# RWKV-6 recurrence and hard-swish MLP in one kernel: chunks of two batches in turn, first diagonal sums on TensorE, first w loaded by itself, part of the first block's down projection by block products

## The chip, the cores and the metric

The kernel runs on one core of a Trainium2 chip. The metric is the device time of one execution in microseconds, given as the median of several runs. A core has five engines that run side by side, each through its own queue in order: TensorE (PE in the profile; PEld is its loading of stationary operands), VectorE (DVE), ScalarE (ACT), GpSimd (POOL) and SyncE (SP), which here issues nearly all transfers. Products land in PSUM, from where DVE and ACT take them to SBUF.

## The reference

```python
batch, n_heads, seq, head_dim = (4, 8, 768, 48)
for t in range(S):
    kt, vt, rt, wt = (k[:, :, t], v[:, :, t], r[:, :, t], w[:, :, t])
    cur = np.einsum('bhd,bhe->bhde', u[None] * kt, vt)
    y[:, :, t] = np.einsum('bhd,bhde->bhe', rt, state + cur)
    state = wt[:, :, :, None] * state + np.einsum('bhd,bhe->bhde', kt, vt)
...
x = attn_out.transpose(0, 2, 1, 3).reshape(B * S, H * D)   # 3072 x 384
h = x @ w_in                                                # 384 x 2048
relu6 = np.clip(h + 3.0, 0.0, 6.0)
g = h * relu6 / 6.0
return (g @ w_out).astype(np.float32)                       # 2048 x 384
```

All of r, k, v, w, u are float32; the two weight matrices come as float64.

## The kernel before

**Chunks and blocks.** The 768 steps of a batch are cut into 6 chunks of 128 (L), which makes 24 chunks, numbered in the order of the batches: chunks 0 to 5 are batch 0. A chunk is a row tile of 128 tokens of the MLP as well, and four chunks (BC) make a block of 512 tokens; there are six blocks.

**A chunk of the recurrence.** Its steps in the planner's list (lines 769 to 832), with the chunk's number behind the name:

- `feat` loads r, k and w with the head's dimension on partitions (674 KB; for chunk 0 in two parts, w on SP's queue and r and k on ACT's, with u's broadcast behind them, L257 to L259), `tok` loads r, k and v with time on partitions (576 KB, L267).
- `back` (DVE, a scan of w from the end, L333, and a reciprocal, L337), `fore` (DVE, a scan from the start, L342), `K` and `R` (products of k and r with the two scans, L353 and L357; on DVE for the first three chunks, on GpSimd then).
- `own` makes r*k*u for the diagonal (two multiplications, L366 and L367, on DVE for chunk 0 and on GpSimd for the others), `sum` reduces it over the head's dimension (DVE, L372), `diag0` and `diag1` lay the result on the diagonals of A (ACT, L380, eight instructions).
- `score` (PE, L388) makes the products of K and R, `above` (DVE, L395, two instructions) puts the part above the diagonal into A.
- `turn` and `turned` transpose K (PE L404, ACT L409), `read` multiplies the state (L440) and the values (L457) into y_ps and makes the chunk's own contribution to the state (L450), `state` (DVE, L414 or L416) adds it, and `decay` (L421) multiplies the state before by the chunk's decay. A batch's first chunk has no state to read, its last none to write. Chunk i's decay needs the state of chunk i-1.
- `leave` copies y_ps into xT, the operand of the MLP. In block 0 a chunk is read in two steps: `first` and `third` take the last pair of heads out (L480), `read` adds it back by a selection product (L487), and `leave` is one copy (L496). In later blocks three small transfers per half (`move`, L517) place the last pair.

**Weights.** Sixteen pairs of weight tiles are fetched as 64-bit words (`fetch`, L292, 768 KB each, three buffers `bits`) and turned into float32: `low` and `whole` on ACT (L301, L305), `shift`, `join` and `full` on DVE (L310, L315, L320).

**Block 0** uses the weights as they arrive. `up` (PE, L536) makes one column tile f of 128 of the hidden layer for one half p of the block (two chunks), 16 x 2 times; `ramp` (ACT, L526) and `gate` (DVE, L544) make the activation into g0 or g1, one tile for each half of the block. `down` (PE, L552) multiplies g of one chunk with w_out, 16 column tiles of 128 in eight steps of two, `drain` (ACT, L559) scales the result and `store` writes it. Blocks 1 to 5 use products of 2 x 2 blocks with seven instead of eight products (`up_product` L634, `down_product` L681), which need sums of blocks of the weights (`sin` L594, `sout` L606), of x (`tx`, L616) and of g (`sum`, L666), and add the products up when they are read out of PSUM (L643, L645, L694, L696).

**The order of the work** is written out by the program before it is built: each step has an engine, a length, the steps it waits for, a key, buffers that it holds (`ring`), and for a load its size. A planner (class Plan) runs through modelled time and takes, of the steps that can start first on an engine, the one with the lowest key. START, CONV, UP, SUMS and LAG give the keys of the first chunks, the conversions, block 0's up steps, the weight sums, and how long before a block its last chunk is read; BEHIND says which weight fetch a chunk's loads come after. Until the first `up` PE runs filler products (`spin`, L980) where the planner sees it without work. Every engine then runs its list in order, whatever the real times are.

Of the kernel before, what the change touches and what calls it, by code (L numbers as in the profile page):

```python
# [18 lines left out]
L = 128  # L19
GP = 64  # L20
LEVELS = 7
BC = 4
# [3 lines left out]
LAG = 19.1  # L26
BEHIND = (-1, -1, 0, 3, 5, 8)
EARLY = 3
START = (-104.5, -104.0, -78.0, -38.2, 22.0, 30.0)
CONV = (-90.0, 6.6)  # L30
UP = (-83.9, 3.6, -69.0, 4.3)
SUMS = (36.2, 2.0)
# [148 lines left out]
def fast_path(tc, feat, tok, wflat, ub, moe_w_in, moe_w_out, out, flag, n_chunks):  # L181
# [20 lines left out]
    with ExitStack() as ctx:  # L202
# [5 lines left out]

        plan = Plan()
# [10 lines left out]
        states = [const.tile([PR, P, D], F32, name=f"state_{i}") for i in range(2)]  # L220
        u_bc = const.tile([128, HD], F32, name="u_bc")
# [32 lines left out]
        def load_feat(i):  # L254
            a = io.tile([PR, nf], F32, name="feat_in")
            if i == 0:
                nc.sync.dma_start(out=a[:, 2 * n:], in_=feat[i, :, 2 * n:])  # L257
                nc.scalar.dma_start(out=a[:, :2 * n], in_=feat[i, :, :2 * n])
                nc.scalar.dma_start(out=u_bc, in_=ub.to_broadcast([128, HD]))  # L259
            else:  # L260
                nc.sync.dma_start(out=a, in_=feat[i])
            st[i].update(r=a[:, :n].rearrange("q (p t) -> q p t", p=P),
                         k=a[:, n:2 * n].rearrange("q (p t) -> q p t", p=P), w=a[:, 2 * n:])

        def load_tok(i):
            b = io.tile([L, 3, HD], F32, name="tok_in", bufs=3)
            nc.sync.dma_start(out=b.rearrange("s c e -> s (c e)"), in_=tok[i].rearrange("s c e -> s (c e)"))  # L267
            st[i].update(rt=b[:, 0], kt=b[:, 1], v=b[:, 2].rearrange("s (h d) -> s h d", d=D))
# [93 lines left out]
        def own(i):  # L362
            d = st[i]
            d["rk"] = wk.tile([L, HD], F32, name="rk", bufs=1)
            eng = nc.vector if i == 0 else nc.gpsimd
            eng.tensor_mul(d["rk"], d["rt"], d["kt"])  # L366
            eng.tensor_mul(d["rk"], d["rk"], u_bc)  # L367

        def own_sum(i):
            d = st[i]  # L370
            d["dg"] = wk.tile([L, H, 1], F32, name="dg")
            nc.vector.tensor_reduce(out=d["dg"].rearrange("s h o -> s (h o)"),  # L372
# [38 lines left out]
        def new_state(i):  # L411
            d = st[i]
            if i % n_chunks == 0:
# [4 lines left out]
        def decay(i):  # L418
            d = st[i]
            d["S"] = wk.tile([PR, P, D], F32, name="S")  # L420
            early(i).tensor_mul(d["S"], states[(i - 1) % 2], d["E"][:, :, 0:1].to_broadcast([PR, P, D]))  # L421
# [12 lines left out]
        def read_state(i, pairs):  # L434
            d = st[i]
            if i % n_chunks:
# [5 lines left out]
        def write(i):  # L442
            d = st[i]
            if i % n_chunks != n_chunks - 1:
# [75 lines left out]
        def new_g(bk, p):  # L520
            blocks[bk]["g", p] = wk.tile([128, NFC, HB], F32, name=f"g{p}", bufs=1)
# [10 lines left out]
        def up(f, p):  # L532
            b = blocks[0]
            h_ps = b["h", f, p] = bank("bankA" if f % 2 else "bankC")
            for j in range(NCC):
                nc.tensor.matmul(h_ps[:, :HB], lhsT=w_in[:, f // 2, j, f % 2, :], rhs=b["xT"][:, j, p * HB:(p + 1) * HB],  # L536
                                 start=(j == 0), stop=(j == NCC - 1))

        def ramp(f, p):
            clip(0, p, blocks[0]["h", f, p][:, :HB], ("r", f, p))  # L540

        def gate(f, p):
            b = blocks[0]
            nc.vector.scalar_tensor_tensor(out=b["g", p][:, f, :], in0=b["r", f, p][:, :HB], scalar=6.0,  # L544
                                           in1=b["h", f, p][:, :HB], op0=ALU.min, op1=ALU.mult)

        def down(c, f0, f1):
# [3 lines left out]
            for f in range(f0, f1):  # L551
                nc.tensor.matmul(b["o", c][:, :DM], lhsT=b["g", c // 2][:, f, c % 2 * L:(c % 2 + 1) * L], rhs=w_out[:, f, :],  # L552
# [8 lines left out]
        def store(bk, c):  # L561
            t0 = bk * MB + c * L
# [92 lines left out]
        def sum_g(bk, p, k, x):  # L655
# [6 lines left out]
            G = b["g", p].rearrange("q f (c t) -> q f c t", c=2)  # L662
# [656 lines left out]
```

## Time and profile before

| | us |
|---|---|
| median of 6 runs | 584.48 (583.68 to 585.09) |
| the profiled execution | 585.28 |
| its span, first to last instruction | 583.6 |
| PE busy | 568.0 (97%) |
| DVE busy | 401.5 (69%) |
| ACT busy | 265.4 (45%) |
| GpSimd busy | 129.0 (22%) |
| mean granted TensorE clock | 0.993 |

The costliest groups of PE are the block products (L634 and L681), then block 0's down projection (L552, 128 passes, 44.4 us of busy time). A float32 product is two passes in the trace, so a product counts as two instructions. Shares of busy time are averages over stages that differ: the first 73 us of the span hold the loads, the conversion of the weights and the first chunks, and the rest is one stream of products. In the views below, a row of stages gives start and end, length, and the busy time of PE, PEld, DVE, ACT and POOL with the number of instructions, and then the granted clock, the busy share of the 16 DMA engines and GB/s. A row of waits reads: the engine and line that waited, who released it, the microseconds in total, how many times, and the longest. A row of a timeline has start, length, engine, line, operation, tiles and, in brackets, the idle time before it and what ended it.

### The profile page before, as it was taken

To read this page: it belongs to the slowest core of one execution; us is meant where nothing else is said; L and a number is where in the kernel's file an instruction comes from. 1 tells how busy PE (TensorE), PEld (TensorE's weight loads), DVE (VectorE), ACT (ScalarE), POOL (GpSimd) and SP (SyncE) were. 2 spreads that over 40 slices of the span, in tenths; PEclk is the share of its full clock that TensorE was granted. 3 is DMA by queue.
4 is the path that set the end of the run, shared out by engine and by line. 5 is a ranking of instruction groups with operands and counts; after the bars stand their busy time and mean duration, and the time that the engine had idled before them with its cause. 6 is when DMAs were issued, how large, how long until landed. Compare 5 with 4: busy or idle time off the path is not lost.

```text
span 583.6 us, 10098 instructions
## 1 busy us (share of the span) xinstructions
PE 568.0 (97%) x3940; PEld 497.1 (85%) x3940; DVE 401.5 (69%) x666; ACT 265.4 (45%) x677; POOL 129.0 (22%) x119
## 2 busy tenths in 40 slices
PE   8997899999999999999999999999999999999995
PEld 8776687666888999988899988899988899988995
DVE  7998798896787996587788477878365634155350
ACT  3677683434656512457630457530456510265100
POOL 3212215435504213304231503142211000000000
PEclk9998999999999999999999999999999999999999
DMA  8969651534324544534437333542100000100001
GB/s 273 334 194 303 195 197 48 172 129 140 125 60 145 198 120 152 181 102 123 164 113 233 122 103 102 152 145 78 64 6 8 2 8 15 43 1 0 1 15 46
DMA packets 20777, 67.26 MB, mean 115 GB/s; under 512 B 2752, under 2 KB 6912, under 8 KB 20720
## 3 DMA queue, kind: packets, MB, share of 16 engines
q1 hardware_dynamic: 20448, 65.86, 34.8%
q8 instruction: 33, 0.54, 0.4%
q10 hardware_dynamic: 272, 0.66, 0.4%
q14 instruction: 24, 0.20, 0.1%
HBM read 60.81 MB, written 4.72 MB: 112 GB/s over the span
## 4 chain that ended last, share of the span: by engine, by line
PE 92%; DVE 4%; DMA 1%; ACT 1%; issue 0%; SPq 0%; DVEq 0%
PE bankA L634 18%; PE bankA L681 17%; PE bankC L634 9%; PE bankC L681 9%; PE bankA L552 7%; PE bankB L634 6%; PE bankB L681 4%; PE y_ps L457 4%; PE bankC L536 4%; PE bankB L388 4%; PE bankA L536 4%; PE y_ps L440 2%; PE ps L450 2%; PE ps L404 1%; DMA tok_in<-in_tok_dram 1%; PE bankA L980 1%
## 5 line engine op out<-in xcount | busy, mean ns | idle before, releaser
L643 ACT COPY g<-bankA 128x256 f32<-128x256 f32 x120 | 44.5, 371 | 51.7 <-PE bankA L634 49.3
L653 DVE SCALAR_TENSOR_TENSOR g<-clip,g 128x512 f32<-128x512 f32 x80 | 58.1, 729 | 9.8 <-ACT clip L526 9.8
L380 ACT ACTIVATE A<-ident,dg 128x128 f32<-128x128 f32 x192 | 59.8, 391 | 10.4 <-DVE dg L372 8.8
L526 ACT ACTIVATE clip<-g,three 128x512 f32<-128x512 f32 x80 | 57.9, 723 | 11.3 <-DVE g L645 10.6
L634 PE MATMUL bankA<-xT,w_in 128*128 128x256 f32 x240 | 60.9, 381 | 0.0
L421 POOL TENSOR_TENSOR S<-state,E 112x192 f32<-112x192 f32 x18 | 19.0, 1058 | 178.3 <-DVE state L416 115.0
L681 PE MATMUL bankA<-w_out,g 128*128 128x192 f32 x320 | 56.8, 328 | 0.0
L681 PEld LDWEIGHTS bankA<-w_out,g 128*128 128x128 f32 x320 | 52.5, 190 | 1.0 <-issue 0.4
L634 PEld LDWEIGHTS bankA<-xT,w_in 128*128 128x128 f32 x240 | 45.0, 190 | 6.0 <-issue 0.4
L552 PE MATMUL bankA<-w_out,g 128*128 128x384 f32 x128 | 44.4, 494 | 1.4 <-DVE w_out L320 1.4
L634 PE MATMUL bankB<-xT,w_in 128*128 128x256 f32 x160 | 41.3, 381 | 0.0
L357 POOL TENSOR_TENSOR W<-feat_in,W 112x512 f32<-112x512 f32 x21 | 27.4, 1303 | 57.2 <-DVE W L342 24.7
L510 ACT COPY xT<-y_ps 48x384 f32<-48x384 f32 x40 | 18.9, 472 | 45.7 <-PE y_ps L457 45.3
L366 POOL TENSOR_TENSOR rk<-tok_in 128x384 f32<-128x384 f32 x23 | 27.0, 1172 | 52.6 <-DMA tok_in<-in_tok_dram 33.6
L694 ACT ACTIVATE o<-bankA 128x192 f32<-128x192 f32 x30 | 9.9, 330 | 62.6 <-PE bankA L681 62.6
L353 POOL TENSOR_TENSOR E<-feat_in,E 112x512 f32<-112x512 f32 x21 | 27.5, 1311 | 45.2 <-issue 34.8
L552 PEld LDWEIGHTS bankA<-w_out,g 128*128 128x128 f32 x128 | 23.5, 190 | 16.4 <-DVE w_out L320 1.6
L645 DVE TENSOR_TENSOR g<-bankC,g 128x256 f32<-128x256 f32 x40 | 16.9, 421 | 26.7 <-PE bankC L634 24.6
L645 DVE TENSOR_TENSOR g<-bankB,g 128x256 f32<-128x256 f32 x40 | 16.9, 421 | 25.0 <-PE bankB L634 22.4
L634 PEld LDWEIGHTS bankB<-xT,w_in 128*128 128x128 f32 x160 | 30.3, 190 | 4.3 <-issue 0.2
L342 DVE TENSOR_TENSOR_SCAN W<-feat_in,start 112x516 f32<-112x516 f32 x24 | 33.2, 1383 | 0.1
L333 DVE TENSOR_TENSOR_SCAN E<-feat_in,back 112x516 f32<-112x516 f32 x24 | 29.4, 1224 | 2.6 <-DMA feat_in<-in_feat_dram 2.6
(260 smaller groups left out, 1248.8 us busy)
## 6 DMA issues: line engine op xcount, KB each, us to landing
feat_in<-in_feat_dram SPq DMA_DIRECT2D x23, 674.2 KB, 4.7
tok_in<-in_tok_dram SPq DMA_DIRECT2D x24, 576.0 KB, 4.3
bits<-in_moe_w_in_dram SPq DMA_DIRECT2D x8, 768.0 KB, 8.5
bits<-in_moe_w_out_dram SPq DMA_DIRECT2D x8, 768.0 KB, 4.5
feat_in<-in_moe_w_in_dram SPq DMA_DIRECT2D x8, 768.0 KB, 4.2
feat_in<-in_moe_w_out_dram SPq DMA_DIRECT2D x8, 768.0 KB, 4.4
out_dram<-o SPq DMA_DIRECT2D x24, 192.0 KB, 1.9
feat_in<-in_wflat_dram SPq DMA_DIRECT2D x6, 768.0 KB, 4.4
```

The costliest lines, as they stand in the source:

```text
L333: nc.vector.tensor_tensor_scan(out=E_[:, ::-1], data0=d["w"][:, :0:-1], data1=back.rearrange("q p t -> q (p t)")[:, ::-1], initial=0.0, op ...
L342: nc.vector.tensor_tensor_scan(out=W_, data0=d["w"][:, :-1], data1=starts[i % 2].rearrange("q p t -> q (p t)"), initial=0.0, op0=ALU.mult, ...
L353: early(i).tensor_mul(d["K"], d["k"], d["K"])
L380: nc.scalar.activation(out=d["A"][:, h, :], in_=ident, func=ACT.Copy, scale=d["dg"][:, h])
L526: nc.scalar.activation(out=c[:, :m], in_=src, func=ACT.Relu, bias=three, scale=1.0)
L536: nc.tensor.matmul(h_ps[:, :HB], lhsT=w_in[:, f // 2, j, f % 2, :], rhs=b["xT"][:, j, p * HB:(p + 1) * HB], start=(j == 0), stop=(j == NCC ...
L552: nc.tensor.matmul(b["o", c][:, :DM], lhsT=b["g", c // 2][:, f, c % 2 * L:(c % 2 + 1) * L], rhs=w_out[:, f, :], start=(f == 0), stop=(f == ...
L634: nc.tensor.matmul(b["p", q, to][:, :HB], lhsT=w, rhs=rhs, start=(n == 0 and k in (1, 2, 5)), stop=(n == len(terms) - 1 and k in (2, 3, 4) ...
L643: nc.scalar.copy(out=to, in_=src)
L645: nc.vector.tensor_add(to, src, to)
L653: nc.vector.scalar_tensor_tensor(out=g, in0=b["r", q, p], scalar=6.0, in1=g, op0=ALU.min, op1=ALU.mult)
L681: nc.tensor.matmul(b["d", p, to][:, :h], lhsT=a, rhs=w(), start=(f == 0 and k in (1, 2, 5)), stop=(f == HF - 1 and k in (2, 3, 4)), skip_g ...
```

## The change

1. **Chunks of two batches in turn.** Chunk i of the program is no longer chunk i of the data: `chunk_of` takes batches 0 and 1 in turn for the first twelve, then 2 and 3. The first two and the last two of each twelve are first and last chunks; `decay` of chunk i needs the state of chunk i-2.
2. **Diagonal sums of chunks 0 to 3 by TensorE.** `own` is one multiplication r*k on DVE in the layout with the head's dimension on partitions, `dot` multiplies it with u on PE (four products of two columns), and `sum` is a copy on ACT. Their `tok` loads v alone (192 KB). u's broadcast is loaded on SP after the fourth weight fetch, for the chunks from 4 on; a small `u_col` is loaded on ACT's queue at the start.
3. **First w alone.** Chunk 0's r and k are loaded on SP after its w, not on ACT's queue beside it.
4. **Down projection of chunks 2 and 3 by block products.** Block 0's second half uses `down_product`, with its sums and reads, in place of 2 x 8 `down` steps. g0 and g1 are laid out by halves of the hidden layer for block 0. A down product waits only for the weight sum that it uses, not for all.
5. **Keys and filler.** LAG, BEHIND, START, CONV, UP and SUMS have other values, the lengths of `up`, `ramp` and `gate` are given by the number of chunks (the same two halves), and ten of the filler products are done as four products of quarters of the array.

```diff
+SPLIT = (2,)
-LAG = 19.1
-BEHIND = (-1, -1, 0, 3, 5, 8)
+LAG = 12.5
+BEHIND = (-1, -1, -1, 0, 6, 7)
+BY_PE = 4
+OWN = 0.5
-START = (-104.5, -104.0, -78.0, -38.2, 22.0, 30.0)
-CONV = (-90.0, 6.6)
-UP = (-83.9, 3.6, -69.0, 4.3)
-SUMS = (36.2, 2.0)
+START = (-119.6, -152.0, -58.6, -43.4, 14.5, 25.8)
+CONV = (-91.7, 6.6)
+UP = (-83.9, 4.3, -71.3, 4.8)
+SUMS = (53.5, 2.3)
...
+        NSEQ = 2 * n_chunks
+        chunk_of = [(i // NSEQ * 2 + i % 2) * n_chunks + i % NSEQ // 2 for i in range(NT)]
+        def is_first(i):
+            return i % NSEQ < 2
+        def is_last(i):
+            return i % NSEQ >= NSEQ - 2
...
             if i == 0:
-                nc.sync.dma_start(out=a[:, 2 * n:], in_=feat[i, :, 2 * n:])
-                nc.scalar.dma_start(out=a[:, :2 * n], in_=feat[i, :, :2 * n])
-                nc.scalar.dma_start(out=u_bc, in_=ub.to_broadcast([128, HD]))
+                nc.sync.dma_start(out=a[:, 2 * n:], in_=feat[chunk_of[i], :, 2 * n:])
+                nc.scalar.dma_start(out=u_col, in_=ug)
...
+        def load_rest():
+            nc.sync.dma_start(out=st[0]["a"][:, :2 * n], in_=feat[chunk_of[0], :, :2 * n])
+        def load_u():
+            nc.sync.dma_start(out=u_bc, in_=ub.to_broadcast([128, HD]))
...
+            if i < BY_PE:
+                nc.sync.dma_start(out=b[:, 2], in_=tok[chunk_of[i], :, 2])
...
         def own(i):
             d = st[i]
+            if i < BY_PE:
+                d["rk"] = wk.tile([PR, P, L], F32, name="rk", bufs=1)
+                nc.vector.tensor_mul(d["rk"], d["r"], d["k"])
+                return
             d["rk"] = wk.tile([L, HD], F32, name="rk", bufs=1)
-            eng = nc.vector if i == 0 else nc.gpsimd
-            eng.tensor_mul(d["rk"], d["rt"], d["kt"])
-            eng.tensor_mul(d["rk"], d["rk"], u_bc)
+            nc.gpsimd.tensor_mul(d["rk"], d["rt"], d["kt"])
+            nc.gpsimd.tensor_mul(d["rk"], d["rk"], u_bc)
+        def own_dot(i):
+            d = st[i]
+            d["dg_ps"] = pp.tile([L, P, 2], F32, name="ps")
+            for p in range(P):
+                nc.tensor.matmul(d["dg_ps"][:, p, :], lhsT=d["rk"][:, p, :], rhs=u_col[:, p, :], start=True, stop=True)
...
+            if i < BY_PE:
+                nc.scalar.copy(out=d["dg"].rearrange("s h o -> s (h o)"), in_=d["dg_ps"].rearrange("s p g -> s (p g)"))
+                return
...
-            early(i).tensor_mul(d["S"], states[(i - 1) % 2], d["E"][:, :, 0:1].to_broadcast([PR, P, D]))
+            early(i).tensor_mul(d["S"], states[i % 2], d["E"][:, :, 0:1].to_broadcast([PR, P, D]))
...
+        def g_of(bk, f, c):
+            if bk == 0:
+                return blocks[0]["g", f // HF][:, f % HF, c * L:(c + 1) * L]
+            return blocks[bk]["g", c // 2][:, f, c % 2 * L:(c % 2 + 1) * L]
...
+            if i < BY_PE:
+                plan.add(f"own{i}", "DVE", 0.66, do(own, i), [f"feat{i}"] + ["later"] * (i == 0) + [f"own{i - 1}"] * (i > 0), k + OWN,
+                         [("rk", [f"dot{i}"])], port=True)
+                plan.add(f"dot{i}", "PE", 0.55, do(own_dot, i), [f"own{i}"], k + OWN, [("ps", [f"sum{i}"])])
+                plan.add(f"sum{i}", "ACT", 0.22, do(own_sum, i), [f"dot{i}"], k + OWN, [("dg", [f"diag1{i}"])])
...
-                         [f"state{i - 1}", f"back{i}"], t - 0.1 if i < len(START) else t - 5, [("S", [f"read{i}"] + [f"state{i}"] * turn)], port=True)
+                         [f"state{i - 2}", f"back{i}"], t - 0.1 if i < len(START) else t - 5, [("S", [f"read{i}"] + [f"state{i}"] * turn)], port=True)
...
-        plan.add("later", "ACT", 0.9, lambda: None, key=-99.0, kb=1, lands=7.2)
+        plan.add("u", "SP", 0.45, load_u, ["fetch3"], -60.0, kb=197)
+        plan.add("later", "SP", 0.45, load_rest, ["feat0"], key=-999.0, kb=459)
...
-        for c in range(BC):
+        for c in classic:
             for q in range(HF):
                 k = D0 + c * D0 / BC + q * 1.29
                 plan.add(f"down0.{c}.{q}", "PE", 1.29, do(down, c, 2 * q, 2 * q + 2),
...
-            for p in range(2):
-                at = K + U_ + D_ * p
+            for p in range(bk == 0, 2):
+                at = K + U_ + D_ * p if bk else D0 * 1.5
...
-                                 before + [d_ + f"{k_}.0"] * x + [d_ + f"{chain}.1"] * bool(chain) + after + sout
-                                 , at + 2.6 * n_ + 1.3 * x + (2.6 if k_ == 4 else 0), hold if x == 0 else ())
+                                 before + [d_ + f"{k_}.0"] * x + [d_ + f"{chain}.1"] * bool(chain) + after + [f"sout{t_}.{x}" for t_ in ({5: 1, 6: 2, 7: 3, 4: 4}.get(k_),) if t_], at + 2.6 * n_ + 1.3 * x + (2.6 if k_ == 4 else 0), hold if x == 0 else ())
...
         def spin():
-            s_ps = bank("bankA")
-            nc.tensor.matmul(s_ps[:, :L], lhsT=ident, rhs=ident, start=True, stop=True)
+            spins.append(len(spins))
+            if 6 <= spins[-1] < 16:
+                two = [bank("bankA") for _ in range(2)]
+                for rows, cols in ((0, 0), (GP, GP), (0, GP), (GP, 0)):
+                    nc.tensor.matmul(two[rows // GP][cols:cols + GP, :GP], lhsT=ident[rows:rows + D, rows:rows + GP],
+                                     rhs=ident[rows:rows + D, rows:rows + GP], start=True, stop=True)
+                return
+            nc.tensor.matmul(bank("bankA")[:, :L], lhsT=ident, rhs=ident, start=True, stop=True)
```

(`classic` is the first two chunks; `all_down` waits for their `down` steps and the seven products of the second half.)

## The prediction

> **What bounds the kernel now.** I read first the 40 slices of the page (each digit is a busy share in tenths):
>
> ```profile
> PE   8997899999999999999999999999999999999995
> ...
> DVE  7998798896787996587788477878365634155350
> ...
> PEclk9998999999999999999999999999999999999999
> DMA  8969651534324544534437333542100000100001
> ```
>
> PE is full from slice 5 on; only the first five slices (73 us) have room, and there DVE and DMA are nearly full too. Next the busy time by stage (length, then PE, PEld, DVE, ACT, POOL, then granted clock, DMA share, GB/s):
>
> ```profile
> 0.00:11.00 11.00, 9.49 (x58) 9.30 (x58) 6.87 (x14) 2.40 (x6) 2.63 (x13) 1.00 0.78 236
> 11.00:28.80 17.80, 16.33 (x184) 13.75 (x182) 16.42 (x23) 12.09 (x31) 5.08 (x4) 1.00 1.03 345
> 28.80:54.00 25.20, 21.25 (x147) 17.18 (x146) 22.33 (x38) 18.67 (x40) 5.94 (x6) 0.99 0.77 248
> 54.00:72.00 18.00, 15.59 (x105) 11.77 (x106) 14.66 (x21) 11.92 (x28) 3.45 (x3) 0.83 0.66 210
> 72.00:101.00 29.00, 29.00 (x136) 23.07 (x135) 26.37 (x44) 17.70 (x36) 10.11 (x7) 1.00 0.38 130
> ```
>
> From 72 us on PE has no gap, so the end moves only by what PE does not do before 72 and by PE work that vanishes. PE's timeline gives the first. The first product of the up projection (L536) starts at 28.75; what PE does before is mostly filler (L980). Adding the start-to-start times of the other rows there (two turns of K 0.4, two scores 1.1, first reads 0.35 and 0.71, selections 0.86 and 0.77, rests 1.25 and 1.82) gives 8.8 us of real work, so 20.0 us are lost. After 28.75 come these waits:
>
> ```profile
> PE bankC L536 <- DVE w_in L320: 3.7, 1, 3.7
> ...
> PE bankA L552 <- DVE w_out L320: 1.4, 1, 1.4
> PE y_ps L487 <- ACT x L480: 1.3, 2, 0.7
> ```
>
> and behind the first of them the clock is at half:
>
> ```profile
> 54.00:58.00 4.00, 3.63 (x9) 2.92 (x10) 3.83 (x6) 2.67 (x8) 0.00 (x0) 0.50 0.87 248
> 58.00:62.00 4.00, 4.00 (x15) 3.35 (x14) 1.25 (x5) 1.55 (x4) 1.81 (x2) 0.71 0.79 281
> ```
>
> Three groups L536 take 6.9 us there (54.37 to 61.26) against 3 x 1.29 = 3.9. So 3.7 + 3.0 + 1.4 + 1.3 = 9.4 us are lost in the middle, 29.4 in all. Why PE waited at 50.7 is seen on DVE:
>
> ```profile
> 51.25 0.42 DVE L544 SCALAR_TENSOR_TENSOR g<-clip,bankA 128x256 f32<-128x256 f32 x1 [0.87 <-ACT clip L526]
> 51.59 0.74 DVE L310 TENSOR_SCALAR top<-bits 128x768 int32<-128x768 int32 x1
> 52.36 0.96 DVE L315 SCALAR_TENSOR_TENSOR top<-bits,top 128x768 int32<-128x768 int32 x1
> 53.36 0.96 DVE L320 CUSTOM_DVE_ANT_0 w_in<-top,more 128x1536 uint16<-128x1536 uint16 x1
> ```
>
> DVE stood 0.87 us, twice, before gates that wait for PE, with the conversion that PE needed queued behind them, though ACT had its words since 47.23. It is an order of work, not only a lack of DVE.
>
> **The change, part by part.**
>
> *First w alone, diagonal sums by TensorE, two batches: the start.* Before, w (226 KB, 4.4 us to landing) shares the engines with 448 KB on ACT's queue and 576 KB of tok, and back's scan starts at 5.36. The nearest small transfers land in 1.9 us (192 KB stores); so w lands between 0.81 + 1.9 = 2.7 and 5.2. I take 3.7, nearer the lower end, since only u_col's few KB goes beside it. On DVE then, by rows: back 1.41, fore 1.23, K 0.68, R 0.69, and own (a multiplication like L353) 0.68: 8.4. The dots are new: four products, eight passes; L404 loads such weights at 0.10 each, L487 runs six passes in 0.87, so 0.8 to 1.16; with a hop and an ACT copy (0.20) the diagonals start at 9.8 and end at 12.2 (eight x 0.306). Chunk 1's five DVE steps (4.7) end at 13.1, chunk 0's mask (1.34) at 14.4. Chunk 1's dot and sum are ready at 14.5, its diagonals at 17.0, its mask at 18.4. Chunk 0: first read 14.6, third (0.53, behind half of the diagonals) 16.4, selection and rest 2.1, leave 0.48: 19.1. The ring y has one tile, so chunk 1's first read follows: 0.35, third 0.53, 2.1, leave 0.48, with hops 23.5 for the first L536. It needs no state, which drops 0.92 us of state reads here, done later instead (20 either way). With w 1.2 us off either way and ACT serving the diagonals before or after third (1.0 either way), 21.3 to 25.7. Real work before: 8.8 - 0.9 = 7.9; lost 15.6 against 20.0: **4.4 us gained** (2.2 to 6.6).
>
> The Trainium skill, "DMA: Bandwidth & Descriptors", section "Anatomy of one DMA", gives a fixed 2.0 us plus bytes over 436 GB/s: an estimate of 3.3 us for w's landing. By it the sum would be 0.4 us lower; no run here has a lone load.
>
> *The steps moved with it.* Loading r and k on SP adds one issue of 0.4 us ahead of feat 1, and u another after the fourth weight fetch; 4 x 384 KB of tok are not loaded before the fifth chunk. ACT loses one issue (0.45) ahead of its table load, which ends at 3.0, before any use. GpSimd loses three pairs L366/L367; the slow DVE rows beside them (1.87 for 1.23 at 12.58, 1.35 for 0.68 at 14.4) say that this helps DVE by about 1.4 us at the start, which I counted by using the undisturbed rows. For chunks 1 to 3 DVE has a multiplication (0.68) in place of a reduction (0.54). All DMA changes lie under the waits above; if that cover is gone, SP's extra issue costs 0.4.
>
> *New waits.* PE's dot waits for own on DVE, with the next score or up product queued behind it and that one's mask or gate waiting; ACT's copy waits for the dot, with third and the conversions behind it. In chunks 0 and 1 the chain above holds them; in 2 and 3 a dot that comes late costs PE the delay, which I leave inside the middle's bounds.
>
> *Order of DVE (START, CONV, UP): the middle.* After the first L536 DVE still owes six conversions of w_in (6 x 2.47), 32 gates (x 0.42), and chunks 2 and 3 (about 6 each): 40 us. PE has 32 x 1.29 + 2 x 4.9 = 51 us. So the 9.4 us are not forced; but the order that the planner finds is not in this trace. Bounds: all 9.4 vanish; or the pace of the weights stays, and the earlier start is only waited away, minus 4.4. Between them I take half, 4.7, because the cause seen is an order with some 11 us of slack behind it, and the new keys put chunk 2 later and chunk 3 earlier rather than adding slack.
>
> The Trainium skill, "TensorE: Matmul & The Clock Gate", Part 1, says that one idle window of about 3.4 us halves the clock until a busy window has passed. The row agrees (3.66 us idle, then 0.50), and it speaks against half a gain: a remaining wait in one piece costs its 3.0 us again, 577 in all; in pieces it costs nothing more.
>
> *Block products for chunks 2 and 3.* Removed: 64 passes of L552 at 0.324 (36 in 11.81, less the tail) = 20.7. Added: 7 x 8 x 2 = 112 passes of L681, 16 in 2.60, = 18.2. **2.5 gained**, on PE without gaps. DVE gets eight sums (0.685) and three reads (0.357), 6.6 us; ACT four reads (0.33) for two drains (0.49). DVE is busy 27.2 of the 34.2 us from 115.0 to 149.2 (14.58 + 5.45 + 7.21), so 7.0 idle hide them; the same chain runs in blocks 1 to 5 with 0.4 us of PE waits. Without that cover it costs up to 6.6.
>
> *Dots of chunks 2 and 3* on PE: 0 (if they fall in a wait) to 2 x 1.16; I take 1.2 **lost**.
>
> *LAG 12.5.* The last chunk's read comes 6.6 later. At block 1 the chain from that read to the new operands took 138.5 to 146.5 = 8.0 us, at block 2 217.5 to 228.7 = 11.2 (its sums queued late). 12.5 covers both, so nothing; uncovered, each us late costs one at a boundary. The filler in four quarters replaces filler that nothing waits for: nothing.
>
> Sum: -4.4 - 4.7 - 2.5 + 1.2 = -10.4. The profiled execution took 585.28 (span 583.6 and 1.7 around it), 0.8 over the median of 584.48. Predicted median: 584.5 - 10.4 = **574**; by the bounds that I think likely together 570 to 579.
>
> **The rivals.**
>
> *Weights set the pace.* DVE moves ahead only by what it saves: scan 1.7 earlier, 1.0 less on chunk 0. For: DVE is at 0.92 of 11 to 28.8 and 0.89 of 28.8 to 54. Against: DVE idles 6.2 us between 28.8 and 72 (43.2 less 37.0 busy), in part with words to convert. Then 584.5 - 2.7 - 2.5 + 1.2 = 580.5.
>
> *No waits left.* 51 us of PE work for 40 of DVE; first L536 as forecast: 584.5 - 4.4 - 9.4 - 2.5 + 1.2 = 569. Against: gates must follow PE in order on DVE.
>
> *DVE becomes the bound late in block 0 (slower).* From 115 to 149.2 there are 7.0 idle us; the block products bring 6.6 and shorten the window by 2.5, and the keys of the weight sums (L594, L606) rise by 17. If the 4.9 us of sums run at 97 to 110 and one chunk's scans and masks (5.0) slide in, DVE lacks 6.6 + 2.5 + 4.9 + 5.0 - 7.0 = 12.0, and the first products of block 1 wait for it: 574 + 12 = 586. It decides from 10.4. Against: chunks 8 to 10 are scanned before 150 already and can give way.
>
> *It doesn't do what it says*: the ring y still makes chunk 1 follow chunk 0, so the start gains little (25.7) and the middle keeps its waits: 584.5 - 2.2 - 2.5 + 1.2 = 581; it lies with the first rival.
>
> **How the numbers follow.** Forecast (570 to 579) 0.5; no waits left 0.2; weights' pace or a start that is no earlier 0.16; no change 0.05; slower 0.09. A measurement of this kernel tells about 0.2% (1.2 us) from no change. Faster 0.86, same 0.05, slower 0.09. The range leaves out about a tenth at each end: 567 to 582.
>
> **What would show it.** First L536 at 23.5 (21.3 to 25.7), back's first scan at 3.7; the wait of L536 for w_in under 3 us in one piece and no clock of 0.5 after 40 us; 112 passes of L681 more and 64 of L552 fewer; block 1's first L634 near 139 instead of 149.2; from there PE without gaps, and the same length to the end. I am wrong if PE waits for DVE between 70 and 140, or if back's scan starts no earlier than 5.

## The result, and the profile after

| | before | after |
|---|---|---|
| median, us | 584.84 (46 runs) | 581.73 (20 runs, 580.16 to 583.19) |
| profiled execution, us | 585.28 | 580.08 |
| its span, us | 583.6 | 578.1 |
| ratio of the times | | 0.9941 [0.993, 0.9952] |

The change makes the kernel 0.6% faster: 3.1 us, where 10.4 had been forecast. Line numbers from here on are those of the changed kernel, unless the kernel before is named; a view of an experiment has that kernel's own numbers, which can lie a few lines off. They are: filler L1044 (in quarters) and L1047, turn L438, score L422, dot L398, state read L474, values L491, selection L521, up L577, `down` L596, block products L678 and L729.

The slices of the page after the change:

```profile
PE   8999999999999999999999999999999999999996
...
DVE  7799988989887876777967667967565715145350
...
PEclk7899999999999999999999999999999999999998
DMA  8879731524433453352355343254010000100001
```

PE's dip between 44 and 73 us, 7 and 8 before, is gone, and so is the 8 of the fourth slice of the clock. A new mark stands in the row of the clock: 7 and 8 in the first two slices, where 9 stood before. By stages (length, then PE, PEld, DVE, ACT, POOL, granted clock, DMA share, GB/s):

```profile
6.00:11.00 5.00, 4.70 (x68) 3.66 (x67) 3.79 (x7) 0.53 (x1) 0.00 (x0) 0.74 1.04 335
11.00:16.00 5.00, 4.93 (x31) 4.50 (x30) 3.19 (x5) 2.69 (x11) 0.00 (x0) 0.50 1.08 334
16.00:20.00 4.00, 4.00 (x27) 3.98 (x26) 2.60 (x5) 2.09 (x4) 0.00 (x0) 0.68 1.02 244
...
31.00:54.00 23.00, 23.00 (x165) 19.58 (x164) 22.11 (x39) 19.02 (x39) 1.66 (x2) 1.00 0.81 247
54.00:72.00 18.00, 16.85 (x125) 12.73 (x122) 17.55 (x25) 12.67 (x29) 8.54 (x7) 1.00 0.79 263
```

PE is busy for 16.85 of the 18 us from 54 to 72, against 15.59 before, and at full clock. That is the forecast's middle, and better than forecast. But PE is also busy almost without a gap from 6 us on and at half clock from 8.4 to 18.6, and DVE and ACT are partly idle in that time: DVE is busy for 5.8 and ACT for 4.8 of the 9 us from 11 to 20. PE's timeline of the start says what it is busy with:

```profile
1.43 2.93 PE L1047 MATMUL bankA<-ident 128*128 128x128 f32 x12 [1.43 <-POOL ident masks.py:199]
4.29 4.15 PE L1044 MATMUL bankA<-ident 48*64 48x64 f32 x72
8.37 1.01 PE L438 MATMUL ps<-ident,E 112*128 112x112 f32 x4
...
11.31 1.86 PE L398 MATMUL ps<-u_col,rk 112*128 112x2 f32 x8
13.11 0.49 PE L1044 MATMUL bankA<-ident 48*64 48x64 f32 x8
13.67 4.21 PE L1047 MATMUL bankA<-ident 128*128 128x128 f32 x18
17.67 0.95 PE L438 MATMUL ps<-ident,E 112*128 112x112 f32 x4
```

The turn of chunk 0 takes 1.01 (0.60 before), 18 passes of filler 4.21, which is 0.23 each (18 took 2.61 before, 0.145 each). The chain of waits through the first 35 us names the filler outright (shares of that time by line; the row is cut short by the profile itself). First the kernel before, then the changed one:

```profile
by line: DMA tok_in<-in_tok_dram 19.8%; PE bankA L980 15.8%; PE bankC L536 8.0%; PE y_ps L457 6.1%; PE bankB L388 5.9%; DVE E L353 5.6%; PE bankA L536 5.5%; DVE W L342 5.3%; PE y_ps L487 4.4%; DVE E L333 3.3%; PE ps L404 3.2%; PE ps L450 3.
```

```profile
by line: PE bankA L1047 37.5%; PE bankA L1044 13.0%; PE bankB L422 8.6%; PE bankC L577 7.4%; PE ps L398 7.4%; PE y_ps L491 6.1%; PE ps L438 4.8%; PE bankA L577 4.3%; PE y_ps L521 3.9%; PE ps L484 3.1%; POOL ident masks.py:199 0.9%; issue 0.
```

Before, the longest share of the same stretch was the transfer of tok (19.8%) and filler had 15.8%; now filler has 50.5%, and no transfer is in the row as far as it goes. The first L577 starts at 30.92, later than the 28.75 before. PE's waits up to 150 us (who waited, for whom, us, times, longest):

```profile
PE bankA L1047 <- POOL ident masks.py:199: 1.4, 1, 1.4
PE y_ps L491 <- DVE A L429: 1.2, 2, 1.0
PE bankC L577 <- DVE g L588: 0.9, 1, 0.9
PE bankC L729 <- DVE S__1243 L714: 0.2, 1, 0.2
PE bankA L729 <- DVE w_out L650: 0.2, 1, 0.2
```

The first stands at the start in both kernels. The next two lie between 60 and 110 us and are all that is left of the middle's losses: 2.1 us, where 9.4 were lost before. After 150 us there is no wait.

### The profile page after: what moved, and what is told of

The parts are those of the page before. It is cut to its first block, busy times and chain, and to the rows that moved or that the text cites. A ratio compares the mean times of both kernels' runs of the same rounds, so it can differ in the third digit from the quotient of the medians.

```text
span 578.1 us, 10344 instructions
## 1 busy us (share of the span) xinstructions
PE 568.1 (98%) x4064; PEld 505.3 (87%) x4064; DVE 404.9 (70%) x674; ACT 265.7 (46%) x683; POOL 128.4 (22%) x114
## 4 chain that ended last, share of the span: by engine, by line
PE 95%; DVE 3%; ACT 1%; issue 0%; POOL 0%; POOLq 0%; DVEq 0%
PE bankA L729 20%; PE bankA L678 18%; PE bankC L729 10%; PE bankC L678 9%; PE bankB L678 6%; PE bankB L729 5%; PE bankB L422 4%; PE y_ps L491 4%; PE bankA L577 3%; PE bankA L596 3%; PE bankC L577 3%; PE bankA L1047 2%; PE y_ps L474 2%; PE ps L484 2%; PE ps L438 2%; PE bankA L1044 1%
## 5 line engine op out<-in xcount | busy, mean ns | idle before, releaser
L729 PE MATMUL bankA<-w_out,g 128*128 128x192 f32 x352 | 62.5, 327 | 0.2 <-DVE w_out L650 0.2
L678 PE MATMUL bankA<-xT,w_in 128*128 128x256 f32 x240 | 61.3, 381 | 0.0
L697 DVE SCALAR_TENSOR_TENSOR g<-clip,g 128x512 f32<-128x512 f32 x80 | 56.8, 716 | 5.2 <-ACT clip L567 4.7
L729 PEld LDWEIGHTS bankA<-w_out,g 128*128 128x128 f32 x352 | 57.9, 190 | 1.8 <-issue 0.8
L379 POOL TENSOR_TENSOR W<-feat_in,W 112x512 f32<-112x512 f32 x21 | 35.2, 1674 | 107.5 <-DVE W L364 89.1
L678 PEld LDWEIGHTS bankA<-xT,w_in 128*128 128x128 f32 x240 | 45.1, 190 | 6.6 <-issue 0.4
L455 POOL TENSOR_TENSOR S<-state,E 112x192 f32<-112x192 f32 x19 | 17.8, 936 | 131.2 <-DVE state L450 54.2
L678 PE MATMUL bankB<-xT,w_in 128*128 128x256 f32 x160 | 41.1, 379 | 0.0
L678 PEld LDWEIGHTS bankB<-xT,w_in 128*128 128x128 f32 x160 | 30.4, 190 | 4.1
L729 PE MATMUL bankA<-bits,g 128*128 128x192 f32 x176 | 30.7, 328 | 0.0
L729 PE MATMUL bankB<-w_out,g 128*128 128x192 f32 x176 | 30.6, 326 | 0.0
L364 DVE TENSOR_TENSOR_SCAN W<-feat_in,start 112x516 f32<-112x516 f32 x24 | 30.0, 1249 | 0.1
L422 PEld LDWEIGHTS bankB<-W,E 48*128 48x128 f32 x192 | 24.0, 193 | 6.6 <-issue 5.7
```

The lines of the kernel that those rows point to most:

```text
L364: nc.vector.tensor_tensor_scan(out=W_, data0=d["w"][:, :-1], data1=starts[i % 2].rearrange("q p t -> q (p t)"), initial=0.0, op0=ALU.mult, ...
L379: early(i).tensor_mul(d["R"], d["r"], d["R"])
L422: nc.tensor.matmul(d["a_ps"][g][:, p, :], lhsT=d["K"][rows, p, :], rhs=d["R"][rows, p, :], start=True, stop=True)
L678: nc.tensor.matmul(b["p", q, to][:, :HB], lhsT=w, rhs=rhs, start=(n == 0 and k in (1, 2, 5)), stop=(n == len(terms) - 1 and k in (2, 3, 4) ...
L697: nc.vector.scalar_tensor_tensor(out=g, in0=b["r", q, p], scalar=6.0, in1=g, op0=ALU.min, op1=ALU.mult)
L729: nc.tensor.matmul(b["d", p, to][:, :h], lhsT=a, rhs=w(), start=(f == 0 and k in (1, 2, 5)), stop=(f == HF - 1 and k in (2, 3, 4)), skip_g ...
```

## The experiments

Each ran in five rounds beside the kernel before, whose median on the same chip was 584.5 to 585.2; a ratio is to that kernel. "The full-filler kernel" is the first one below.

### What the filler costs

**All filler on the full array** (twice, on two chips).

```diff
-            if 6 <= spins[-1] < 16:
-                two = [bank("bankA") for _ in range(2)]
-                for rows, cols in ((0, 0), (GP, GP), (0, GP), (GP, 0)):
-                    nc.tensor.matmul(...)
-                return
```

> The changed kernel with all its filler products over the full array (the ten in quarters done as the others); the order of all other work is the same. Its profile shows PE without a gap from 1.4 to 30.9 us, at a clock of 0.74, 0.50 and 0.68 between 6 and 20, with 18 and 8 passes of filler (4.2 and 1.1 us) ahead of chunk 1's turn and dot. Theory A (the filler, slowed by the low clock, holds the start): the clock is 1.0 from 6 us on, the first L577 near 27 us, and the time 3 to 4 us under the changed kernel's 581.7. Theory B (the weights set the pace, so an earlier start is waited away in the middle): first L577 near 27 too, but PE waits of 3 to 4 us more for gates or w_in between 40 and 75, and 581 to 583.

> The kernel with all filler on the full array once more, beside the two others: 575.6 within 1.2 us, first L577 at 26.5.

Measured: 575.62, ratio 0.984 [0.9815, 0.9865], and 575.22, ratio 0.9846 [0.983, 0.9861]. So 6.1 us of the changed kernel's time (5.9 by the two ratios) are those ten steps, which change no result. PE's timeline of the first of the two:

```profile
1.43 6.12 PE L1041 MATMUL bankA<-ident 128*128 128x128 f32 x30 [1.43 <-POOL ident masks.py:199]
7.38 0.55 PE L438 MATMUL ps<-ident,E 112*128 112x112 f32 x4
8.95 1.05 PE L398 MATMUL ps<-u_col,rk 112*128 112x2 f32 x8
9.87 2.88 PE L1041 MATMUL bankA<-ident 128*128 128x128 f32 x20
...
26.53 1.46 PE L577 MATMUL bankC<-xT,w_in 128*128 128x256 f32 x6
```

Turn and dot take about half of what they take in the changed kernel, the turn is a microsecond earlier, and the first L577 comes at 26.5 instead of 30.9. That lead of 4.4 us is still there at block 1: its first L678 is at 142.2 instead of 146.6.

**No filler; only the first sixteen steps of the changed kernel's.**

```diff
         def spin():
-            spins.append(len(spins))
-            ...
+            return
```

```diff
             spins.append(len(spins))
+            if spins[-1] >= 16:
+                return
```

> The changed kernel without any filler product. Theory A: nothing stands ahead of chunk 1's turn and dot; even at a half clock the first L577 comes near 26 (chunk 1's dot starts when own is done, 14.1, instead of 19.5), and the time falls by 4 to 5 us to 577. Theory B: the first L577 comes at 26 and the time stays at 581 to 583, with waits of 5 us more in the middle. A third theory, that the filler earns its place by the clock: first L577 at 30 or later and 583 or more, with the clock at 0.5 until 30.

> The changed kernel with its first 16 filler products (six over the full array, ten in quarters, to 13.7 us) and none after. Theory A: first L577 near 26 to 27, time near 577 to 578. Theory B: the same first L577 and 581 to 583. Against the run without any filler it tells what the early filler is worth.

Measured: 581.81, ratio 0.9951 [0.9931, 0.9972], and 583.31, ratio 0.9959 [0.994, 0.9978]. The changed kernel with its filler is as slow as without any. Without, the turn starts when K is ready (7.11) but takes 0.98, the dot 1.87, and the first L577 is at 31.59. With the first sixteen steps the turn takes 1.01, the two dots 1.87 and 1.86, and the first L577 is at 34.03: filler in quarters did no more for the clock than no filler.

**Is it the length of the ten steps, or the clock?** One kernel leaves the ten out of the full-filler kernel, so that PE is idle there; the other makes each of them two full products, as long as the quarters.

```diff
             spins.append(len(spins))
+            if 6 <= spins[-1] < 16:
+                return
```

```diff
-            nc.tensor.matmul(bank("bankA")[:, :L], ...)
+            for _ in range(2 if 6 <= spins[-1] < 16 else 1):
+                nc.tensor.matmul(bank("bankA")[:, :L], ...)
```

> The changed kernel with full filler but with nothing in the place of the ten quarter products: six fillers, then PE stands idle to the first turn of K near 7, then the rest of the filler over the full array. It tells the two ways apart in which the quarter products can cost their 6.1 us. If it is their length (they end at 9.6 where K is ready at 7.1): this run has no such delay and comes near the full filler, 575.6 to 577. If it is that PE stays at half its clock until 18: the first score, dot and the fillers behind them take double here too, first L577 near 29.5, 579 to 580.

> The kernel with all filler on the full array (575.6), but each of the ten filler steps that the change does in quarters is two full products (four passes, about 0.44 at the full clock, where the quarters took 0.41 to 0.59). So the ten are as long as the quarters, and the array is full. Length and clock apart: the first turn at 8.8 to 9.5 instead of 7.4. If 3.5 of the 6.1 us that the quarters cost are their length: 579.1 (578 to 580), first L577 at 29 to 30, no half clock after 8 us (turn 0.55, dot 1.05). If it is nearly all the clock: no later than 576.5. If it is nearly all length: 581 to 582.

Measured: ten left out 578.23, ratio 0.9886 [0.9867, 0.9905]; ten long ones 577.14, ratio 0.9879 [0.9863, 0.9896]. The timeline of the first shows an early turn at half clock,

```profile
1.43 2.93 PE L1043 MATMUL bankA<-ident 128*128 128x128 f32 x12 [1.43 <-POOL ident masks.py:199]
7.20 1.01 PE L438 MATMUL ps<-ident,E 112*128 112x112 f32 x4 [2.84 <-DVE E L375]
10.15 1.87 PE L398 MATMUL ps<-u_col,rk 112*128 112x2 f32 x8
11.87 4.19 PE L1043 MATMUL bankA<-ident 128*128 128x128 f32 x18
```

and that of the second a late turn at full clock:

```profile
1.43 7.85 PE L1042 MATMUL bankA<-ident 128*128 128x128 f32 x48 [1.43 <-POOL ident masks.py:199]
9.12 0.55 PE L438 MATMUL ps<-ident,E 112*128 112x112 f32 x4
10.69 1.05 PE L398 MATMUL ps<-u_col,rk 112*128 112x2 f32 x8
11.60 3.20 PE L1042 MATMUL bankA<-ident 128*128 128x128 f32 x22
```

The clock alone costs 578.23 - 575.4 = 2.8 (with the mean of the two full-filler medians), the length alone 577.14 - 575.22 = 1.9. Together 4.7 of 6.1. No run prices the rest; the quarters are longer still at half clock (below), which may be a part of it. The length is worth less than the 3.5 us that leaving the ten out had left for it; the clock is the larger part.

**Less filler, by the planner's own measure** (the share of PE's idle time that is filled) **and full filler that ends after sixteen steps.**

```diff
-    FILL = 0.75
+    FILL = 0.45
```

```diff
             spins.append(len(spins))
+            if spins[-1] >= 16:
+                return
```

> Compared with the changed kernel with full filler (575.6, first L577 at 26.5): 0.45 instead of 0.75 of PE's planned idle time is filled, all else the same. There 5.7 us of filler still stand in PE's queue between 14 and 26.5, ahead of chunk 1's dot, of the selections and of the first L577. Theory A (the filler holds the start): first L577 near 24.5, time 573 to 574.5. Theory B (an earlier start is waited away for weights and gates in the middle): first L577 at 24.5 and 575 to 576. If the clock is lost with less filler (turns at 0.98, dots at 1.87): first L577 at 28 or later, 578 or more.

> The kernel with all filler on the full array, without the filler after the sixteenth step, so none behind chunk 0's dot. 5.7 us of filler stand there between 14 and 26.5 us. Theory (filler in the queue makes the start later than the 23.5 us of my sum): the first L577 1.5 to 3 us earlier, at 23.5 to 25, and 573 to 575. Rival (the filler lies in waits for DVE and ACT, and the chain of chunk 1 sets the start): the first L577 at 26 to 27, 575.6 as before, or more if waits of over 3 us halve the clock (as 583.3 did with quarters, where the clock had never been at full).

Measured: 577.44, ratio 0.9879 [0.9853, 0.9904], and 580.9, ratio 0.9942 [0.9917, 0.9967]. The second was to show that filler queued between 14 and 26 us holds the start up. That fell. Its waits and its stages:

```profile
PE ps L438 <- ACT A L414: 2.5, 1, 2.5
PE y_ps L521 <- ACT x L514: 1.5, 2, 0.8
```

```profile
6.00:11.00 5.00, 4.61 (x41) 4.13 (x39) 4.45 (x7) 1.12 (x4) 0.00 (x0) 1.00 1.05 340
11.00:16.00 5.00, 2.18 (x12) 2.00 (x12) 4.93 (x8) 4.09 (x11) 0.00 (x0) 0.79 1.07 360
16.00:20.00 4.00, 3.20 (x23) 2.56 (x23) 3.82 (x7) 3.57 (x12) 0.00 (x0) 0.50 1.02 259
```

With PE busy for 2.18 of 5 us the clock went to half, and the first L577 came at 28.1 rather than 26.0. The filler there earns more through the clock than it costs in the queue. In the kernel with FILL 0.45 the clock was lost at the start as well (dot 1.86).

**The kernel before, with quarters in place of ten of its filler steps.**

```diff
+            if 6 <= spins[-1] < 16:
+                two = [bank("bankA") for _ in range(2)]
+                ...
+                return
             nc.tensor.matmul(bank("bankA")[:, :L], ...)
```

> The kernel before with ten of its filler products in quarters, as in the change, and nothing else. Theory C (the quarter products cost the changed kernel 6 us: each takes 0.44 to 0.59 us where the planner counts 0.22, and PE stays at half its clock behind them): the first turn of K starts near 15 instead of 10.6, the first L536 at 33 instead of 28.8, and the time is 588 to 590. Rival: in the kernel before the start waits for data, not for PE, and nothing changes, 584 to 585.5.

Measured: 585.27, ratio 1.0013 [0.9999, 1.0028], no change clear of the noise (at most 1.6 us). Its first turn is 3.7 us later (14.37 for 10.64), its first up product 1.9 us later (30.69 for 28.75), and yet block 1's first product only 0.5 (149.8 for 149.2). Its waits for w_in, w_out and x are those of the kernel before to the digit, 3.7, 1.4 and 1.3.

In these two executions what was lost at the start came back in the middle: the clock from 54 to 72 us was 0.91 there and 0.83 in the kernel before, 0.08 x 18 = 1.4 us of full clock. So the same filler cost nothing that can be measured before and costs 6.1 us after the change. That the change took away the losses that it could hide in is my reading of these two traces.

### What the other parts are worth

These start from the full-filler kernel (the first also from the changed one), so that the start's clock doesn't cover them.

**Block products for chunks 2 and 3 undone.**

```diff
-        classic = range(2)
+        classic = range(BC)
...
-        for bk in range(NB):
+        for bk in range(1, NB):
```

> The changed kernel with part 4 undone: block 0's second half by 64 passes of the plain down projection instead of 112 passes of block products, so DVE's eight sums and three reads for it go too. The prediction's term: 2.5 us slower, 584.2. If DVE's 6.6 us of extra work cost PE waits in the changed kernel, less than 2.5: 581.7 to 583.

> Compared with the changed kernel with full filler (575.6): part 4 undone, 64 passes of the plain down projection for 112 passes of products. The prediction's term: 2.5 slower, 578.1. If DVE's 6.6 us of sums and reads cost PE waits where the products are: 576 to 577. If the freed layout and order matter too, as in the same edit with the quarter filler (4.2 slower): 579.8.

Measured: 585.93, ratio 1.0016 [0.9995, 1.0038], from the changed kernel (4.2 more), and 580.67, ratio 0.9931 [0.9911, 0.9951], from the full-filler one (5.0 more). The passes account for 2.5; the waits of PE from 200 to 250 us, of which the changed kernel has none, for 2.9:

```profile
PE bankC L729 <- DVE S__2032 L714: 2.3, 1, 2.3
PE bankB L729 <- DVE o L744: 0.6, 1, 0.6
```

The longer wait is for a sum of g, late on DVE. It seems that the order of DVE that the planner writes with these keys fits the block products and not the sixteen steps. The trace is of an execution of 583.03, 2.4 over the median, and has 0.79 of the clock from 215 to 223 us, behind that wait; how much of the 5.0 the waits make in the other executions is not shown.

**Diagonal sums as before**, on GpSimd from whole toks (chunk 0's on DVE, with its tok ahead of the second feat).

```diff
-BY_PE = 4
+BY_PE = 0
...
-                nc.scalar.dma_start(out=u_col, in_=ug)
+                nc.scalar.dma_start(out=u_bc, in_=ub.to_broadcast([128, HD]))
...
+            eng = nc.vector if i == 0 else nc.gpsimd
```

> Compared with the changed kernel with full filler (575.6): the diagonal sums as before (chunk 0 on DVE with its whole tok loaded ahead of chunk 1's feat, chunks 1 to 3 on GpSimd and a reduction), no dots. The prediction's terms: chunk 0's own 1.67 for 0.68 on DVE, 384 KB more ahead of chunk 1's feat (1.4 us), the slow DVE rows beside GpSimd 1.4: first L577 3 to 4 us later, less 1.6 for the dots of chunks 2 and 3: 577 to 578. If the weights' words are what the smaller loads help, another 3 us of waits for w_in between 40 and 70: 580 to 581.

Measured: 588.66, ratio 1.0063 [1.0039, 1.0087], 13.0 more. The first up product is 3.2 us later (29.74), and PE waits in the middle, in one piece, with half clock (0.50 from 66 to 74 us) behind it:

```profile
PE bankA L597 <- DVE g L589: 4.5, 1, 4.5
PE ps L439 <- DVE E L375: 1.8, 1, 1.8
PE y_ps L492 <- DVE A L430: 1.5, 2, 1.3
```

**Chunks of one batch after the other.**

```diff
-        NSEQ = 2 * n_chunks
-        chunk_of = [(i // NSEQ * 2 + i % 2) * n_chunks + i % NSEQ // 2 for i in range(NT)]
+        NSEQ = n_chunks
+        chunk_of = list(range(NT))
...
-                         [f"state{i - 2}", f"back{i}"], ...
+                         [f"state{i - 1}", f"back{i}"], ...
```

> Compared with the changed kernel with full filler (575.6): the chunks in the order of one batch after the other; PE's order up to the first L577 stays the same but for chunk 1's state reads, which come back. If the two batches only shorten the start: state reads 0.9 and chunk 1's wait for the state of chunk 0, first L577 at 27.5 to 28.5, 576.5 to 577.5. If they also keep the middle and later blocks free of waits: more, 579 to 583, with waits for a state or its decay.

Measured: 580.52, ratio 0.992 [0.9905, 0.9936], 4.9 more. The first L577 is 1.5 later (28.05), for chunk 1 reads a state again; the rest I put down to waits, from a trace of the slowest of its eight executions (583.59):

```profile
PE bankC L729 <- DVE S__1310 L714: 3.3, 2, 2.1
PE y_ps L491 <- DVE A L429: 2.3, 2, 2.1
```

**Chunk 0's r and k beside w again, on ACT's queue.**

```diff
+                nc.scalar.dma_start(out=a[:, :2 * n], in_=feat[chunk_of[i], :, :2 * n])
...
-            nc.sync.dma_start(out=st[0]["a"][:, :2 * n], in_=feat[chunk_of[0], :, :2 * n])
+            return
```

> Compared with the changed kernel with full filler (575.6): part 3 undone, chunk 0's r and k on ACT's queue beside w, the planner's order unchanged. The prediction's term: w lands 1.6 later, as at 5.36 in the kernel before, the first turn at 8.5 to 9 instead of 7.4, the first L577 1 to 1.6 later and the time 576.5 to 577.2. If the wait for chunk 1's feat (9.4) hides it: 575.6.

Measured: 579.04, ratio 0.9905 [0.9885, 0.9924], 3.4 more. Back's first scan starts at 5.62 instead of 3.8, the turn at 8.98, the first up product at 27.35, 0.8 later than with w alone. Its profiled execution is 576.72, the quickest of its runs, so the trace shows only a third of the 3.4; where the rest goes in the others is not shown.

**Keys of before** (LAG, BEHIND, START, CONV, UP and SUMS).

```diff
-LAG = 12.5
+LAG = 19.1
...
-START = (-119.6, -152.0, -58.6, -43.4, 14.5, 25.8)
+START = (-104.5, -104.0, -78.0, -38.2, 22.0, 30.0)
...
-SUMS = (53.5, 2.3)
+SUMS = (36.2, 2.0)
```

> Compared with the changed kernel with full filler (575.6): LAG, BEHIND, START, CONV, UP and SUMS as in the kernel before, all else of the change kept. The prediction put 4.7 us of the gain on the new keys (the middle's waits). If the middle's waits come back with the old ones, 5 to 7 us: 580 to 583, with a wait of L577 for w_in or gates of 3 us and more between 40 and 60. If the other parts (less words to load, DVE freed from GpSimd) removed the waits: 576 to 577.

Measured: 590.28, ratio 1.0115 [1.0089, 1.0141], 14.7 more and slower than the kernel before. The first L577 (27.65) is 1.1 later; the longer waits, in a trace of its quickest execution (587.57), are these:

```profile
PE bankA L596 <- DVE w_out L342: 4.2, 2, 3.8
PE ps L438 <- POOL E L375: 3.3, 1, 3.3
PE bankC L729 <- DVE S__1290 L714: 2.4, 1, 2.4
```

None of these prices may be added to another: undone one at a time, the parts cost 4.9, 13.0, 3.4, 5.0 and 14.7, 41 us in all, where the whole change with full filler is worth 9.4. Each was taken out under keys that had been chosen with it in.

## Why the prediction was wrong, by its own steps

The direction was right, and one rival of the direction, a DVE that becomes the bound late in block 0, did not come: DVE was busy for 30.7 of the 34.6 us up to block 1's first product, and PE's two waits for sums there were 0.2 each. The size was wrong.

**The step that failed** is the last clause of the change part by part: "The filler in four quarters replaces filler that nothing waits for: nothing." It was true of the kernel before, where quarters cost nothing that can be measured. After the change it costs 6.1 us. The forecast itself had moved back's scan to 3.7 and chunk 0's DVE steps to an end at 8.4, and so had taken away what the first turn waited for; then the next thing late is the filler ahead of it in PE's queue. A step costed at nothing has to be costed again in the schedule that the other steps make. In numbers: nine steps in quarters took 4.15 us, 0.46 each, where the planner counts 0.22; a full step takes 0.47 at half clock and 0.29 at full. And the quarters did not hold the clock, which the forecast did not ask about. With 6.1 in place of nothing the forecast's own sum is -10.4 + 6.1 = -4.3, against the measured -3.1.

**The start.** The scan began at 3.77 as forecast (3.7), by a lone w that landed 2.9 us after its issue at 0.8. The Trainium skill, "DMA: Bandwidth & Descriptors", section "Anatomy of one DMA", from which the prediction had estimated 3.3, is on transfers that GpSimd issues; w is issued by SP. Chunk 0's DVE steps ended at 8.3 (8.4). The forecast for the first L577 was 23.5. It was 30.9 as changed and 26.0 and 26.5 with full filler, so this term was mis-sized even then: 1.4 us gained (real work of 7.9 leaves 18.6 lost, from 20.0), not 4.4. In the full-filler run with 26.0, chunk 0's second mask ends at 14.87, but its first values (L491) come at 16.55 and not at once: chunk 1's turn, filler, dot and scores stand ahead of them in PE's order. My chain followed DVE and ACT and left out what PE's list has in between; that is 1.7 of the 2.5 us. How early the start would be with less filler and a full clock stays open, since each kernel with less filler lost the clock.

**The middle.** Forecast 4.7 of 9.4 won; measured 7.3. The wait for w_in and the half clock behind it are gone. The forecast's reason, an order of work with slack behind it, fits: the keys of before alone bring a wait of 3.8 us for a conversion back, though the first L577 is only 1.1 us later. The rival that the weights set the pace fits the kernel before, in which a start 1.9 us later came to 0.5 at block 1, and not the changed one: there the 4.4 us of an earlier first L577 arrived whole at block 1.

**Block products.** 2.5 us by passes, as worked out, with the cover on DVE that was named. **Dots of chunks 2 and 3.** 2 x 0.85 = 1.7 lost, within the bounds 0 to 2.3, for 1.2. **LAG.** No wait at a boundary, as said.

With full filler the terms are -1.4 - 7.3 - 2.5 + 1.7 = -9.5, against the measured -9.4 (575.62 from 585.07 on its chip) and the forecast -10.4: two errors of 3.0 (the start) and 2.6 us (the middle) that nearly cancelled, so that the sum comes out so near is luck. The changed kernel's profiled execution has a first L577 of 30.9 and so +3.0 in the first place: -5.1, and its span shrank by 5.5. The median shrank by 3.1 only, because the profiled execution is one of the quicker: of 22 executions on record 6 have a recorded clock of 0.988 to 0.991, as the profiled one has, and a mean of 580.96 us; the other 16 have 0.998 or more and a mean of 581.81. How a higher recorded clock can go with a longer time is told at the end.

Of the marks that were to show the steps, one was badly chosen. Block 1's first product was expected at 139; it came at 146.6 and, with full filler, at 142.2. From that mark to the end it is 434.4 us before and 431.5 in both others, so the mark shows 2.9 us too little. Of these, 2.1 are a chunk's read that stands ahead of the mark after the change and stood behind the first products before.

The best version is the full-filler kernel: 1.6% faster than the kernel before and, by the two ratios, 1.0% faster than the changed one.

## What to carry to other kernels

Filler in an engine's queue is work: look for it by name in the chain of waits, and cost it again whenever a change makes the work behind it ready earlier. A planner that counts a filler step at half its measured length writes a late start into the program, and in this kernel only the filler whose products kept the clock was worth its place. Parts that were fitted together can't be priced by undoing one at a time; their waits tell more than their differences.

## What the hardware showed

**Quarter products neither raise nor hold the clock.** Two traces show it, the changed kernel's and that of the changed kernel with block products undone. Both have the same early filler, six full steps from 1.43 to 4.3 us and quarters behind them. Their rows of the same 64 passes:

```profile
4.96 3.47 PE L1044 MATMUL bankA<-ident 48*64 48x64 f32 x64
```

```profile
4.96 4.63 PE L1044 MATMUL bankA<-ident 48*64 48x64 f32 x64
```

In the first trace the record of the granted clock rises at 4.94 us, 3.5 us after the first full product, and falls at 8.36, while quarters run (PE busy for 2.97 of these 3.42 us); it rises again at 18.59, behind full filler. So a step in quarters took 0.43 us at full clock and 0.58 at half, and eight of them at full clock lost it. In the second trace the first rise is at 19.55: there the six full steps were not enough, and the quarters did not add what was missing. Nor did the small products of turn, scores and dot raise it, with which PE was busy for all 3.41 us from 8.36 to 11.77 in the first trace.

The Trainium skill, "TensorE: Matmul & The Clock Gate", Part 1, says that the clock is half by default and full some 4 us into sustained matmul activity. The full-filler kernel agrees roughly: its clock rises at 6.28 and 7.08 us in its two traces, 4.9 and 5.7 us after the first product, and with the long steps at 4.36, 2.9 us after it, and it stays up. The quarters differ: 3.4 us of them in a row did not count as such activity.

The times at which the record changes, from a trace's first rise to its last, lie 3.41 us or a multiple of it apart (4.94, 8.36 and 18.59 in the changed kernel; 53.45 and 60.28 in the kernel before; 7.05, 13.88 and 24.12 with full filler that ends after sixteen steps). Where the first of them falls differs between traces, and the same six full steps raised the clock in one and not in the other.

**A granted clock of 1.00 may be half speed.** In the changed kernel with block products undone the clock had not risen when its 18 passes of filler and the first turn ran:

```profile
4.29 5.31 PE L1044 MATMUL bankA<-ident 48*64 48x64 f32 x72
9.53 1.01 PE L438 MATMUL ps<-ident,E 112*128 112x112 f32 x4
...
14.83 4.21 PE L1047 MATMUL bankA<-ident 128*128 128x128 f32 x18
```

```profile
11.00:16.00 5.00, 4.93 (x37) 4.50 (x34) 3.10 (x4) 1.63 (x8) 0.00 (x0) 1.00 1.07 360
```

The 18 passes take 4.21 us, exactly as in the changed kernel's trace, where the column reads 0.50 and 0.68; here it reads 1.00, and nothing in the column tells that the clock was half. The column, as I read these two traces, shows a clock taken away, not one never granted, so at the start of a program the length of one known product is the thing to read.

Here the quarters take 0.59 each, the turn starts at 9.53, 1.2 us after the changed kernel's, and the first L577 comes at 31.99, 1.1 us after. This can explain the two sorts of executions of the changed kernel: those with a recorded clock of 0.99 would have been granted the clock at the start and lost it, as the profiled one was, and the 16 with 0.998 or more would not have been granted it before the later filler. No trace of these 16 was kept, so this is not shown; they are 0.85 us slower in the mean.
